# The inner weight's blocks are turned before their norm is summed, and all instructions stand in a new order

## The chip, the cores and the metric

The kernel runs on one core of a Trainium2 chip. The core has five engines that work side by side: PE (TensorE, matrix products), DVE (VectorE), ACT (ScalarE), POOL (GpSimd), and SP (SyncE), which issues nearly all DMA transfers. Each engine executes its own list of instructions in order and waits on semaphores. The metric is the device time of one execution in microseconds.

## The reference, cut to what matters

Three stages follow one another on 2304 tokens (4 batches of 576):

```python
scores = q @ k.T / sqrt(64)               # 4 x 8 heads, 576 x 576
kth    = 32nd largest score of each row
attn   = softmax(where(scores >= kth, scores, -1e9))
x      = (attn @ v)                       # 2304 x 512
h      = x @ w_in                         # 512 -> 2048
x      = (h * sigmoid(1.702 h)) @ w_out   # 2048 -> 512
out    = (((x @ w1) * (x @ w2)) @ w3) @ w_out2   # 512 -> 1024 -> 1024 -> 512
```

The weights arrive as 64-bit floats; q, k and v as 32-bit floats.

## The kernel before

**Tiles and heads.** The tokens are cut into 18 tiles of 128. Each tile has 8 heads, so there are 144 heads (a head below is one tile by one attention head). A head has a fixed course. PE forms its 128x576 scores in one of two PSUM score buffers ("S", line 1122). DVE finds the 32nd largest score of each row by four maxima of eight values (L1142) with three replacements between them (L1145). ACT forms "cut" (L1164) out of the scores and the fourth maximum and by that frees the score buffer; then it takes the exponential (L1167). The result is split into a high and a low half of 16 bits (L1230, L1185), turned by a DMA transpose (L1188), and multiplied with v on PE (L1202, L1204). As there are two score buffers, S of a head waits for the cut of the head two before it. After 8 heads the tile goes through the two gated networks, whose products are L772 to L774: each product of two numbers is made of three 16-bit products of their halves.

**Weights.** They are 72 blocks of 128 x 512: 8 of w_out2 ("w4"), 16 of w3 (1024 x 1024, the inner weight), 16 of w_in, 16 of w_out and 16 of w1 and w2. `load64` brings one block in as 16-bit pieces of the 64-bit numbers (L487; SP), into one of six raw slots. Its highest piece is copied (the "top": ACT L499, POOL L502 or DVE L505), passed into PSUM (the "pass": PE L508 or ACT L511) and joined there with the rest to a 32-bit number by DVE (the "join", L516). The join frees the raw slot, so that the load six blocks later can go out. `l2_scale` sums up a group of blocks with PE: the "gram" (L554, four products per block), its diagonal (L565), and from it a power of two by which the group is scaled. w3 is used in two groups of 8 blocks. `split` makes the high half (L602) and the low half of a scaled block. The low half has several ways: PE takes the high half back into PSUM ("back", L611) and DVE subtracts (L618); or PE forms the difference by two matmuls ("less", L614 and L615) and ACT stores it; or ACT or POOL do it alone (L624, L627, L631).

**The inner weight.** w3 and w_out2 are multiplied together before the first tile needs them: `weights()` turns each joined block of w3 on PE (`turned3`, L683, copied by ACT at L686) and forms the product (L809). The turn waits for the join and for the block's gram, and it is the turn that gives the block's storage back.

**The order.** All operations are registered with an object `Order`, which has for each a list of alternatives (engine and code). A compressed table, `PLAN`, holds for each operation its rank and its chosen alternative; `Order.run` writes the operations out by rank. So the table sets the list of every engine, the loads of SP among them.

```python
o.rank, k = self.plan[len(self.ops)]          # L66
for o in sorted(self.ops, key=lambda o: o.rank):   # L83
```

Of the kernel before, what the change touches and what calls it, by code (L numbers as in the profile page):

```python
# [18 lines left out]
AF = mybir.ActivationFunctionType  # L19
# [18 lines left out]
class Order:  # L38
# [104 lines left out]
PE_DUE, PE_OUT = 100.0, 20.0  # L143
TURN = ("w4", "w3")
# [10 lines left out]
    'c-jq@17jUa07h3cv!mUa-J18tO`4?Xt=%SRn<i~kyGd=^wr$(CZQHiZ_x{6&a}-5YG(}ga;wYJwoQj{Pgc7ZkRG@+sQ^5*TEKdec7LUIY;0abjl`y4{Qc6iw'  # L155
    'YJ2*47I-##aw)l$5GAh?;qiIOdSW~+lt`tBQb|crs(8kE#(SoFiYsN5T1q`7U1{KH=xOTNq@*Y{l)6fDrK{4#v(0nKvrgHioKwy#SCqS+`<~~XV(NC~wsJ@L'
    'tbA3zcnmM_3PmceC##Z2iBj@=3Mv_u?4Cd+Na0E*Pc}~u#iMvV;YvQmP(T@?*h*2Qm=dp~Dm9hHo`If`N}N*1Q{U50DW@cRIxGE@Udk|Ks%M5WRGHwJ?^&cQ'
    'RhB6$JS&wE$`sFHWx3K#>8nih%u!Y=>y-_j{feqGHM2LXT3Riu#(Qh2@03r9?nP>nT32oA?W)#P)6{ft2h~wCdVSua>Qm*V^4{}PiBYR~t9k3G)s<FC8>NHN'
    'Lm8k9Rz@jfm08L><*H(;{gp||TxE;0RoS8JR*oxYm3zu7<-77%X`{APJF7j^-s)g=h&o1{psrNcsCU$7s;$0I2PqSk>&gvfvNBWoplE6~HOTwVyGq%tWKeUc'
    'zZIzFR{hm-YMi&acc-#f2~%U$1Ii&KMQx(CQoDOkdygnbm8t4H^`vr2*{WVv@2gL}nqN<~mwH{jt#(oSs-ILt<636Fv3@tyk7_0@w>C<htQOQ#w5D1szaf4}'  # L160
    'TC&zqOVh@x)70_WG;OA~)9;MmPxZIDQroBPQ7@|dwG-N7?TMc!Fs~ZnE#i$<iJD2x>CL5{P;Po|d7deM6z=tSz3N|8_~rETYBSWC-dWzc>R0ubiu`QNPYqP_'
    'c*E68>Rs<E?`!pfdP{xmeWLDHkEzGKr_}!H0ClJLpn6n2sh;(oSMRAW)i>UEYGEy2OYlq7(zV7~6TcQ(d9|WiNljF1t98@{YD2Y=+D#o+c0{Aujpj6JS9W}('
    'MU56WYF~C-*-m9Am2IvrYt*sPibnogh!&;g*9vH5v>2^|R#B_0)h*XItzKHcw9L`@{qy+y{A+6U)9R#kOsl4~OskRBI_<mqM^!alqnfK_(fqVPEuR*o6-q0X'
    '7M<3noT+!!vgm)bV!G6e>v^>DX+_iG(gtYbv`N}zZHhKqo1-n$)@diTL)vTYnD#}xT+UC2dOrPYxu0pj(tf8|(b@eo_=oySE!eMwUrB9|wo%*Uw^=K#mD8$f'
    ')wQ?k2k#dz(}rmywfWj&t(n@wJKwud?V<Jb8{{`iJFFem&iS3!DrxPs_F5+`yOv9f)QW4pwBFiqzv<d3?V@(c?~Zm=yQV$R9%|dQ9ojCxgIYJOyEa#wr#;o4'
    'YcKs?X;-wH+AZz2c2~QnJ=0!jZ?t#Xd+mevP5bx%oaj2xGwPXij~<}s)eA&d^)KyT&3}Hh9kAFxLqLh>hW@esjr`~6d!koGABYauBhq`N_f3z|E9!;x%6epU'
# [100 lines left out]
def kernel(  # L267
# [840 lines left out]
    def head(t, h, X):  # L1108
# [100 lines left out]
        if h == H - 1:  # L1209
            rel += [("q", qe, "qa"), ("q", qe, "qb")]  # L1210
# [362 lines left out]
```

## Time and profile before

| what | us |
|---|---|
| three runs | 949.43, 949.82, 950.68 |
| median | 949.82 |
| profiled execution, whole | 950.18 |
| its span in the profile | 948.4 |
| PE / DVE / ACT / POOL busy | 921.8 / 865.2 / 724.5 / 785.2 |
| granted TensorE clock, mean of the span | 0.998 of full speed |

The profiled execution lies 0.36 us above the median. The span is what the profiler shows from the first to the last instruction; 1.8 us of the execution lie outside it. PE's 26.6 us without work are the difference between its busy time and the span. Names are those of the program without buffer numbers: `w` is a raw block or a joined one, `win` and `wout` are the storage of the split weights, into which blocks are also joined early; `ysb` and `usb` are work buffers; `mm` and `s_ps` lie in PSUM.

### The profile page before, as it was taken

Reading aid. Unit: us, or ns where it says so; the run is one execution under the profiler, and the core shown is the slowest. Engines: PE = TensorE matmul, PEld = TensorE weight load, DVE = VectorE, ACT = ScalarE, POOL = GpSimd, SP = SyncE. Lnnn points to the kernel's source line nnn. Section 1 sums busy time; section 2 is a strip of 40 time slices with the busy share of each in tenths; the row PEclk is TensorE's granted clock in tenths of the full one; section 3 lists DMA queues with packets and bytes.
Section 4 is the critical chain, followed back from the end, with each engine's and each line's share of the span. In section 5 each row is a group of like instructions: output and inputs, shape, how many; then the busy total and the mean of one; then the engine's idle time right before and its main releaser. Section 6 shows DMA issues by size and latency. Waiting matters only on the chain.

```text
span 948.4 us, 19725 instructions
## 1 busy us (share of the span) xinstructions
PE 921.8 (97%) x6641; PEld 484.6 (51%) x6642; DVE 865.2 (91%) x1838; ACT 724.5 (76%) x1426; POOL 785.2 (83%) x1045
## 2 busy tenths in 40 slices
PE   4799989999999999999999999999999999999998
PEld 2555555555545555555555555554555555544553
DVE  5999999999999999999999999999999999997252
ACT  5899999998879987877888796887776676745231
POOL 3899998999989998999999998989997887856101
PEclk9999999999999999999999999999999999999999
DMA  8999999877987887878895798598675846656201
GB/s 290 321 304 332 298 232 243 180 136 139 160 159 138 163 133 138 145 140 151 142 183 110 141 172 155 100 158 169 123 124 111 161 96 129 118 94 108 44 12 45
DMA packets 397862, 149.31 MB, mean 157 GB/s; under 512 B 375872, under 2 KB 384064, under 8 KB 397760
## 3 DMA queue, kind: packets, MB, share of 16 engines
q1 hardware_dynamic: 397760, 148.05, 75.6%
q8 instruction: 52, 0.85, 0.4%
q14 instruction: 50, 0.41, 0.1%
HBM read 52.41 MB, written 4.72 MB: 60 GB/s over the span
## 4 chain that ended last, share of the span: by engine, by line
PE 82%; ACT 5%; POOL 4%; DVE 3%; DMA 3%; issue 2%; SPq 1%; ACTq 0%; POOLq 0%; DVEq 0%
PE mm L772 23%; PE mm L774 22%; PE mm L773 22%; PE s_ps L1122 7%; PE mm L1204 4%; PE mm L1202 2%; DMA w<-in_moe_w_out_dram 1%; DVE ysb L1145 1%; DVE m8s L1142 1%; ACT mm L511 1%; DMA tsb<-in_moe_w_dram 1%; DMA ysb<-in_k_dram 1%; ACT ysb L1167 1%; PE mm L614 1%; POOL wout L631 1%
## 5 line engine op out<-in xcount | busy, mean ns | idle before, releaser
L1142 DVE MAX8 m8s<-ysb 128x8 f32<-128x576 f32 x432 | 321.5, 754 | 6.3
L1145 DVE MATCH_REPLACE8 ysb<-m8s,ysb 128x576 f32<-128x576 f32 x288 | 213.9, 743 | 0.0
L1185 POOL TENSOR_TENSOR ysb<-ysb 128x512 f16<-128x512 f32 x142 | 164.3, 1160 | 0.3
L1164 ACT ACTIVATE ysb<-s_ps,m8s 128x576 f32<-128x576 f32 x144 | 106.2, 738 | 56.4 <-DVE m8s L1142 45.6
L772 PE MATMUL mm<-w,usb 128*128 128x512 f16 x377 | 142.9, 379 | 0.0
L774 PE MATMUL mm<-w,usb 128*128 128x512 f16 x377 | 142.9, 379 | 0.0
L773 PE MATMUL mm<-w,usb 128*128 128x512 f16 x377 | 142.9, 379 | 0.0
L774 PEld LDWEIGHTS <-usb 128*128 128x128 f16 x824 | 80.6, 98 | 97.2
L1167 ACT ACTIVATE ysb<-ysb,nbs,small 128x576 f32<-128x576 f32 x144 | 123.7, 865 | 5.2 <-POOL nbs L1152 2.3
L772 PEld LDWEIGHTS <-usb 128*128 128x128 f16 x824 | 80.5, 98 | 86.4 <-issue 2.6
L773 PEld LDWEIGHTS <-usb 128*128 128x128 f16 x824 | 80.6, 98 | 82.6
L1142 DVE MAX8 m8s<-s_ps 128x8 f32<-128x576 f32 x144 | 108.6, 754 | 1.8 <-PE s_ps L1122 1.5
L1145 DVE MATCH_REPLACE8 ysb<-m8s,s_ps 128x576 f32<-128x576 f32 x144 | 107.6, 747 | 0.0
L1122 PE MATMUL s_ps<-kts,qts 128*128 128x288 f16 (+1 forms) x640 | 96.7, 291 | 2.1 <-ACT ysb L1164 2.1
L772 PE MATMUL mm<-win,usb 128*128 128x512 f16 x240 | 91.0, 379 | 0.0
L774 PE MATMUL mm<-win,usb 128*128 128x512 f16 x240 | 90.9, 379 | 0.0
L773 PE MATMUL mm<-win,usb 128*128 128x512 f16 x240 | 90.9, 379 | 0.0
L774 PE MATMUL mm<-wout,usb 128*128 128x512 f16 x207 | 78.5, 379 | 0.0
L773 PE MATMUL mm<-wout,usb 128*128 128x512 f16 x207 | 78.4, 379 | 0.0
L772 PE MATMUL mm<-wout,usb 128*128 128x512 f16 x207 | 78.4, 379 | 0.0
L1122 PEld LDWEIGHTS <-qts 128*128 128x128 f16 (+1 forms) x640 | 55.3, 101 | 42.4 <-issue 13.1
L1204 PEld LDWEIGHTS <-ats 128*128 128x128 f16 (+1 forms) x1440 | 68.4, 100 | 9.3 <-issue 4.3
(305 smaller groups left out, 2107.4 us busy)
## 6 DMA issues: line engine op xcount, KB each, us to landing
w<-in_moe_w_out_dram SPq DMA_DIRECT2D x24, 511.8 KB, 5.5
w<-in_moe_w_dram SPq DMA_DIRECT2D x22, 511.8 KB, 5.9
w<-in_moe_w_in_dram SPq DMA_DIRECT2D x16, 511.8 KB, 6.3
qts<-qts SPq DMA_DIRECT2D x34, 128.0 KB, 2.5
ysb<-in_k_dram SPq DMA_DIRECT2D x16, 256.0 KB, 3.6
ysb<-in_v_dram SPq DMA_DIRECT2D x16, 256.0 KB, 2.9
out_dram<-usb SPq DMA_DIRECT2D x16, 256.0 KB, 2.9
usb<-in_q_dram SPq DMA_DIRECT2D x13, 256.0 KB, 3.5
```

Source lines behind the costliest of these rows:

```text
L511: nc.scalar.copy(E["mm"], E["w"].bitcast(BF16)[:, 0:C])
L772: nc.tensor.matmul(o, a[:, i, :], hi, start=(first and i == 0), stop=False)
L773: nc.tensor.matmul(o, a[:, i, :], lo, start=False, stop=False)
L774: nc.tensor.matmul(o, a[:, 4 + i, :], hi, start=False, stop=(last and i == 3))
L1122: nc.tensor.matmul(E["sp"][r : r + n, i], qe[q_][:, h, r : r + n], kt[:, j * S + i * HS : j * S + (i + 1) * HS], start=k_ == 0, stop=k_ == 1,)
L1142: nc.vector.max(out=E["m8"][:, 8 * i : 8 * i + 8], in_=E["sp"] if i == 0 else E["w"])
L1145: nc.vector.match_replace(out=two(E["w"]) if i == 0 else E["w"], in_to_replace=E["m8"][:, 8 * i : 8 * i + 8], in_values=E["sp"] if i == 0 ...
L1164: nc.scalar.activation(two(E["y"]), E["sp"], AF.Prelu, bias=E["m8"][:, TOPK - 1 : TOPK], scale=-1.0, alpha=1.0 / FAR)
L1167: nc.scalar.activation(E["y"], E["y"], AF.Exp, bias=E["nb"], scale=nesc)
L1185: return lambda: eng.tensor_tensor(hl()[:, S + SR : 2 * S], *y_of(at_main, SM), op=ALU.subtract)
L1202: nc.tensor.matmul(o[:, 0:D], at_, v2[:, j_, blk, 0:D], start=False, stop=False)
L1204: nc.tensor.matmul(o[:, 0 : D + 1], at_, v2[:, j_, blk, D : P + 1], start=i == 0, stop=i == 8)
```

## The change

The turn of a w3 block no longer waits for the block's gram but for its join alone. The gram now waits for the turn and gives the block back. All 16 turns are registered ahead of the grams, which is why the grams of a group can stand together behind them. Three alternatives are offered to the table beside this: k, q and the attention weights of the first batches and tiles may be turned on PE (`by_pe`) where a DMA transpose did it. The new table uses this for one transpose of k alone: nine small matmuls (L784 after) and three copies on ACT, and 14 transposes of k by DMA where there were 15. The table itself is new throughout.

```diff
+A_BOTH, Q_BOTH, K_BOTH = 5, 4, 2
@@ PLAN
-    'c-jq@17jUa07h3cv!mUa-J18tO`4?Xt=%SRn<i~kyGd=^wr$(CZQHiZ_x{6&a}-5YG(}ga;wYJwoQj{Pgc7ZkRG@+sQ^5*TEKdec7LUIY;0abjl`y4{Qc6iw'
+    'c-jq@V|yM=13;Ifo!Qx)-Mhver*WF3R@63alQvCir?!o!wr$(CZQHi(zVA;s*L6OeBT0&+Nmw!^F6EN^rMyytR7pydR0&8#G9>D?ym`F&yn#{yDbgDvg-aEr'
...
@@ l2_scale
-                0.235, due - 1000, lambda i=i: f_gram(i), deps=[prev, Es[i]["join"]], env=E, acq=["mm"] if i == 0 else [], tag="gram"
+                0.235, due - 1000, lambda i=i: f_gram(i), deps=[prev, Es[i]["join"], Es[i].get("turn")], env=E, acq=["mm"] if i == 0 else [],
+                rel=[("blk", Es[i], "w")] if "turn" in Es[i] else [], tag="gram"
...
@@ turned3
-        a = pe(0.45, 0.0, f_in, deps=[W["join"], W["gram"]], env=E, acq=["f", "mm"], rel=[("blk", W, "w")], tag="w3 in")
+        W["turn"] = a = pe(0.45, 0.0, f_in, deps=[W["join"]], env=E, acq=["f", "mm"], tag="w3 in")
...
@@ weights
+        e3 = [{} for _ in E3]
+        tr3 = [turned3(W, e) for W, e in zip(E3, e3)]
         g3 = [l2_scale(E3[8 * g : 8 * g + 8]) for g in range(2)]
...
-                e = {}
-                tr = turned3(E3[2 * f + kc], e)
+                e, tr = e3[2 * f + kc], tr3[2 * f + kc]
...
@@ kv_prep
-        last_of["k T"] = dma(
-            1.35, due, f_t, deps=[m], env=E, rel=["kh"], tag="k T", lat=2.4, data=1.40, after=last_of.get("k T")
+        both = b < K_BOTH
...
+            kready[b, hp] += by_pe([piece(0, 4), piece(4, 8), piece(8, 9)], [m, last_of["k T"]], [], [("kh", E, "kh")], "k ")
```

The numbers of lines are higher after the change: load L495, join L524, turn L692, gram L562, S L1191, maximum L1211, replacement L1214.

**SP, the first loads.** SP's list from its start; `in_moe_w_out_dram` is w_out2 here, `in_moe_w_dram` is w3, `w_70` the raw slots. Before:

```order
L1063 DMA w_70<-in_q_dram 128x8x64
L487 DMA w_70<-in_moe_w_out_dram 128x2047
L982 DMA ysb<-in_k_dram 128x2x256
L987 DMA ysb<-in_k_dram 64x64 x2
L487 DMA w_70<-in_moe_w_out_dram 128x2047 x3
L982 DMA ysb<-in_k_dram 128x2x256
L987 DMA ysb<-in_k_dram 64x64 x2
L487 DMA w_70<-in_moe_w_out_dram 128x2047 x2
```

After:

```order
L1113 DMA w_70<-in_q_dram 128x8x64
L495 DMA w_70<-in_moe_w_dram 128x2047
L1023 DMA ysb<-in_k_dram 128x2x256
L1028 DMA ysb<-in_k_dram 64x64 x2
L1023 DMA ysb<-in_k_dram 128x2x256
L1028 DMA ysb<-in_k_dram 64x64 x2
L495 DMA w_70<-in_moe_w_out_dram 128x2047
L495 DMA w_70<-in_moe_w_dram 128x2047
L1023 DMA ysb<-in_k_dram 128x2x256
L1028 DMA ysb<-in_k_dram 64x64 x2
L1113 DMA usb<-in_q_dram 128x8x64
```

The first weight is a block of w3, where the first six were blocks of w_out2. A third piece of k and the q of tile 1 (into `usb`) have moved up, and the rows after hold three weight blocks where the rows before hold six.

**PE, the turns.** The stretch around the first turns, some heads in. `w_70` and `w_71` are joined blocks, `ident` the unit matrix by which a block is turned. Before, the gram (L554) of a block stands ahead of its turn (L683):

```order
L554 LDWEIGHTS w_70
L554 MATMUL mm_91<-w_70 128x128
L683 MATMUL mm_93<-ident,w_71 128x128 x4
L554 LDWEIGHTS w_71
L554 MATMUL mm_91<-w_71 128x128
```

After, turns (L692) stand between passes (L516) ahead of a head's S (L1191), with no gram (L562) yet:

```order
L516 LDWEIGHTS ident
L516 MATMUL mm_90<-w_71,ident 128x512
L692 MATMUL mm_93<-ident,w_70 128x128 x4
L516 LDWEIGHTS ident
L516 MATMUL mm_91<-w_71,ident 128x512
L692 MATMUL mm_92<-ident,w_71 128x128 x4
L516 LDWEIGHTS ident
L516 MATMUL mm_93<-w_71,ident 128x512
L516 LDWEIGHTS ident
L516 MATMUL mm_90<-w_71,ident 128x512
L692 MATMUL mm_91<-ident,w_71 128x128 x4
```

Five turns stand ahead of the first gram of any block; before, seven blocks had their gram ahead of the first turn.

**DVE, the joins.** The stretch among the first heads' maxima, where `s_ps` is a new head's first maximum. Before:

```order
L1145 MATCH_REPLACE ysb<-m8s,ysb 128x576
L516 SCALAR_TENSOR_TENSOR w_71<-w_70,mm_90 128x512
L1142 MAX m8s<-ysb 128x8
L516 SCALAR_TENSOR_TENSOR w_71<-w_70,mm_93 128x512
L1142 MAX m8s<-s_ps_89 128x8
L516 SCALAR_TENSOR_TENSOR w_71<-w_70,mm_92 128x512
L1145 MATCH_REPLACE ysb<-m8s,s_ps_89 128x576
```

After:

```order
L524 SCALAR_TENSOR_TENSOR w_71<-w_70,mm_90 128x512
L1211 MAX m8s<-ysb 128x8
L524 SCALAR_TENSOR_TENSOR w_71<-w_70,mm_91 128x512
L1214 MATCH_REPLACE ysb<-m8s,ysb 128x576
L524 SCALAR_TENSOR_TENSOR w_71<-w_70,mm_90 128x512
L1211 MAX m8s<-ysb 128x8
L524 SCALAR_TENSOR_TENSOR w_71<-w_70,mm_93 128x512
L1211 MAX m8s<-s_ps_88 128x8
L524 SCALAR_TENSOR_TENSOR w_71<-w_70,mm_90 128x512
```

After, the joins stand closer: in 32 rows of DVE's list from the first one shown there are 13 of them, where 32 rows from the first one shown before hold 10.

## Rows read from the trace of the kernel before

**Rows 1.** Part 1 of the page: engine, busy us, share of the span, instructions.

```profile
PE 921.8 (97%) x6641; PEld 484.6 (51%) x6642; DVE 865.2 (91%) x1838; ACT 724.5 (76%) x1426; POOL 785.2 (83%) x1045
```

**Rows 2.** Windows: length; busy PE, PEld, DVE, ACT, POOL; clock; DMA share; GB/s.

```profile
0.00:24.00 24.00, 10.75 (x56) 5.57 (x57) 13.02 (x30) 12.81 (x26) 9.57 (x21) 1.00 0.90 290
24.00:192.00 168.00, 158.43 (x1042) 89.29 (x1043) 163.65 (x381) 161.01 (x318) 154.67 (x207) 0.99 1.03 272
192.00:900.00 708.00, 708.00 (x5297) 368.02 (x5296) 669.13 (x1398) 537.85 (x1062) 615.11 (x811) 1.00 0.74 135
900.00:948.40 48.40, 44.60 (x248) 21.74 (x246) 19.39 (x31) 12.86 (x22) 5.85 (x7) 1.00 0.11 28
```

**Rows 3.** The same view for the first full stretch of heads.

```profile
24.00:48.00 24.00, 19.36 (x124) 13.85 (x124) 23.68 (x56) 21.47 (x46) 20.81 (x28) 0.93 1.04 323
```

**Rows 4.** Timeline 179:184: start, length, engine, line, operation; in brackets its wait.

```profile
179.19 1.41 DVE L1142 MAX8 m8s<-ysb 128x8 f32<-128x576 f32 x2
...
181.14 0.72 ACT L1164 ACTIVATE ysb<-s_ps,m8s 128x576 f32<-128x576 f32 x1
...
181.91 0.65 PE L1122 MATMUL s_ps<-kts,qts 128*128 128x288 f16 x4 [0.20 <-ACT ysb L1164]
...
182.67 0.77 DVE L1142 MAX8 m8s<-s_ps 128x8 f32<-128x576 f32 x1 [0.63 <-PE s_ps L1122]
```

**Rows 5.** Waits of DVE from 17 to 190 us: total, times, longest.

```profile
DVE msm L1303 <- ACT usb L1288: 0.9, 2, 0.7
DVE small L1295 <- ACT small L1294: 0.8, 1, 0.8
...
DVE m8s L1142 <- PE s_ps L1122: 0.6, 1, 0.6
```

**Rows 6.** Timeline of PE, 119.5:121, the gram of two blocks.

```profile
120.01 0.39 PE L554 MATMUL mm<-w 128*128 128x128 bf16 x4
120.24 0.39 PE L554 MATMUL mm<-win 128*128 128x128 bf16 x4
```

**Rows 7.** Timeline of PE, 129:133, preparation of the weights.

```profile
131.00 1.02 PE L614 MATMUL mm<-win,tsb 128*128 128x512 f32 x2
131.86 0.38 PE L615 MATMUL mm<-w,ident 128*128 128x512 f16 x1
132.08 0.38 PE L611 MATMUL mm<-win,ident 128*128 128x512 f16 x1
```

**Rows 8.** DVE by line and form: out<-in, count, busy us, mean ns.

```profile
L1142 DVE MAX8 m8s<-ysb 128x8 f32<-128x576 f32 x432 | 321.5, 754 | 6.3
L1145 DVE MATCH_REPLACE8 ysb<-m8s,ysb 128x576 f32<-128x576 f32 x288 | 213.9, 743 | 0.0
...
L516 DVE SCALAR_TENSOR_TENSOR wout<-w,mm 128x512 uint32<-128x512 uint32 x25 | 16.7, 677 | 0.3 <-issue 0.2
...
L618 DVE SCALAR_TENSOR_TENSOR win<-win,small,mm 128x512 f16<-128x512 f32 x4 | 3.0, 739 | 0.1
...
L426 DVE SCALAR_TENSOR_TENSOR usb<-xsb,msm,usb 128x512 f16<-128x512 f32 x1 | 0.8, 751 | 0.9 <-ACT usb L416 0.9
```

**Rows 9.** Timeline 15:18, up to the first maximum.

```profile
15.58 0.66 ACT L499 CAST w<-w 128x512 f16<-128x512 bf16 x1 [1.07 <-DMA w<-in_moe_w_out_dram]
...
16.90 0.69 DVE L516 SCALAR_TENSOR_TENSOR w<-w,mm 128x512 uint32<-128x512 uint32 x1 [0.74 <-ACT mm L511]
...
17.51 0.76 DVE L1142 MAX8 m8s<-s_ps 128x8 f32<-128x576 f32 x1
```

**Rows 10.** Timeline 910.5:911.2, two engines reading SBUF together.

```profile
910.65 1.19 POOL L1324 TENSOR_TENSOR usb<-psb,usb 128x512 f16<-128x512 f32 x1 [11.71 <-ACT usb L1318]
910.86 1.53 DVE L1324 TENSOR_TENSOR usb<-usb 128x512 f16<-128x512 f32 x1
```

**Rows 11.** Timeline of DVE, 870.5:870.6, the same operation alone.

```profile
870.55 0.69 DVE L1324 TENSOR_TENSOR usb<-usb 128x512 f16<-128x512 f32 x1
```

**Rows 12.** Part 6 of the page: one weight block's load, KB, us to landing.

```profile
w<-in_moe_w_dram SPq DMA_DIRECT2D x22, 511.8 KB, 5.9
```

More of the change, by code (lines that the diff above doesn't have):

```diff
@@ L159 @@
[L159 to L166, printed above, removed]
@@ L252 @@
+    'OVbh'
 )
@@ L763, in turns, with by_pe, f_pe, f_a @@
         return res
+    def by_pe(banks, deps, acq, rel, tag):
+        none = ("N", 0.0, None, 0.0)
+        prev, res = deps[-1], []
+        for k_, (mats, view, dst, n) in enumerate(banks):
+            T = {}
+            def f_pe(T=T, mats=mats):
+                todo = mats(T["b"])
+                for i, (o, w_) in enumerate(todo):
+                    nc.tensor.matmul(
+                        o, w_, upper(ident)[0 : w_.shape[0], 0 : w_.shape[0]], start=i == 0 or (i == 1 and o.shape[0] < P), stop=i == len(todo) - 1, skip_group_check=True
+                    )
+            def f_a(T=T, view=view, dst=dst):
+                nc.scalar.copy(dst(), view(T["b"]))
+            def f_v(T=T, view=view, dst=dst):
+                nc.vector.tensor_copy(dst(), view(T["b"]))
+            c = 0.03 + 0.055 * n * (1 if len(mats.__defaults__ or ()) < 2 else mats.__defaults__[1]) / P
+            prev = op(
+                [none, ("T", c, f_pe, 0.0), ("T", c, f_pe, 0.0)], 0.0, deps=deps + [prev],
+                acq=(list(acq) if k_ == 0 else []) + [("mm", T, "b")], rel=rel if k_ == len(banks) - 1 else [], tag=tag + "turn",
+            )
+            k = n / C
+            res.append(op(
+                [none, ("A", 0.1 + 0.38 * k, f_a, 0.0), ("V", 0.08 + 0.52 * k, f_v, 0.0)], 0.0, deps=[prev], rel=[("mm", T, "b")], tag=tag + "turned",
+            ))
+        return res
     def product_op(due, get, at, w, blocks, first, last, deps, acq, rel, tag):
@@ L1209, in head @@
         if h == H - 1:
-            rel += [("q", qe, "qa"), ("q", qe, "qb")]
+            rel += [("q", qe, x) for x in (("qa", "qb", "qap", "qbp") if qe.get("both") else ("qa", "qb"))]
         s = pe(0.49 if len(pt) == 1 else 0.62, due - 1000 - 8, f_s, deps=qhalf[t, h // 4] + kd + [last_of.get("S")], env=E, acq=["sp"], rel=rel, tag="S")
@@ L1243, in head, with part, mats @@
         else:
-            tr = [dma(1.35, due + 8, f_t, deps=[lo], env=E, acq=["at"], rel=["hl"], tag="a T", lat=2.4, data=1.40, after=last_of.get("a T"))]
+            both = t < A_BOTH
+            none = ("N", 0.0, None, 0.0)
+            tr = [op([("D", 1.35, f_t, 0.0)] + [none] * (2 * both), due + 8, deps=[lo], env=E, acq=["at"], rel=["hl"], tag="a T", lat=2.4, data=1.40, after=last_of.get("a T"))]
+            if both:
+                def part(i0, i1):
+                    def mats(t_):
+                        return [(t_[:, (i - i0) * P : (i - i0 + 1) * P], hl()[:, i * P : (i + 1) * P]) for i in range(i0, i1)]
+                    return mats, lambda t_: t_[:, 0 : (i1 - i0) * P].rearrange("p (k m) -> p k m", m=P), lambda: E["atp"][:, i0:i1], (i1 - i0) * P
+                tr += by_pe([part(0, 4), part(4, 8), part(8, 9)], [lo, tr[0]], [("at", E, "atp")], [("hl", E, "hl")], "a ")
+                E["both"] = True
         last_of["S"], last_of["a hi"], last_of["a T"] = s, hi, tr[0]
@@ L1250, in head @@
                 0.845 if len(pt) == 1 else 1.0, due - 1000 + 10, f_av, deps=X["tr", h - 1] + tr + [last_of.get("av")] + vd,
[L1251 removed]
+                acq=[("mm", X, ("av", hp))] + ([("x", X, "x")] if hp == 0 else []), rel=[("at", z, k_) for z in (X["E", h - 1], E) for k_ in (("at", "atp") if z.get("both") else ("at",))] + rel, tag="av",
             )
```

225 lines of the change are left out of this document (131 added, 94 removed).

## The prediction

> **What bounds the kernel now.** I read part 1 of the page first. PE works 921.8 us of a span of 948.4 [rows 1], so 26.6 us of idle PE are all that an order can give back without taking work away. The windows say where these lie [rows 2]: 13.25 us in the first 24, 9.57 in the 168 up to 192, none at all in the 708 from there to 900, and 3.80 in the tail. From about 192 on PE is never out of work, so the end is set by two things: when that state is reached, and how much PE work is then left.
>
> What holds PE up before is read from the timeline around its last wait [rows 4]. S of the 23rd head starts at 181.91 and waited for the cut of the 21st, which frees a score buffer. The cut started at 181.14, though DVE had ended the 21st head's fourth maximum at 179.9 (the first of the two at 179.19, half of 1.41 each): a hand-off of 2.0 us, mostly ACT busy with other things. DVE then took up the new scores at 182.67 after 0.63 of waiting. DVE works 163.65 of the 168 us of that window [rows 2], and 23.68 of the first 24 of them, while PE works 19.36 [rows 3]; its waits between 17 and 190 are few, the largest 0.9 for ACT in two pieces, 0.8 for ACT, 0.6 for S [rows 5]. So up to the 23rd head the heads go at DVE's pace, and PE fills the gaps between the S of one head and the next with weight work. PE work moved ahead of that S is hidden; PE work moved behind it is paid in full.
>
> **The sum, at the S of the 23rd head.** I count instructions ahead of it in both orders and price them from the trace.
>
> PE ahead of that S. A 128x512 product of 16 bits takes 0.22 (131.86 to 132.08), a "less" of three matmuls 1.08 (131.00 to 132.08) [rows 7]; a small 128x128 matmul 0.057, by the eight of two grams (120.01 to 120.24 for four) [rows 6]. After the change there are 9 small matmuls more for k (+0.51), 8 backs fewer (-1.73), 2 lesses fewer (-2.16), 7 passes more (+1.51) and six matmuls fewer of a tile product (-1.30): -3.17 us. Over the whole program PE has 8 passes more (+1.73), 8 backs fewer (-1.73), one less fewer (-1.08) and the 9 small ones: -0.57. So behind that S there are 2.60 us more PE work than before: +2.6 on the end, if S comes at the same time. The 3.17 taken from the front only make longer gaps there.
>
> DVE ahead of that S, from its first maximum of all to the fourth of the 21st head, with the work before it: 2 maxima more at 0.754, 2 replacements more at 0.743, 2 joins fewer at 0.677, 7 subtractions behind a back fewer at 0.739, and 3 subtractions more that read both operands from SBUF, at 0.751 of the one such row [rows 8]; with a 0.72 and a 0.74 more of the first gate and the inner product, one 0.68 of turned q fewer and some small ones (-0.27, estimates by the same rows): 1.51 + 1.49 - 1.35 - 5.17 + 2.25 + 0.78 - 0.27 = -0.8. It is not all gain, for ACT and POOL take over what DVE gives up; I take -0.6.
>
> The start. The first maximum comes at 17.51, directly behind a join at 16.90 [rows 9]. Before the change 6.29 us of DVE work lie ahead of it, after it 5.61. The early w3 block stands behind 3.5 MB of loads. In the trace a top that waited for its load stood behind 3.75 MB and started at 15.58 [rows 9]; 3.5 MB in proportion to the 323 GB/s of the stretch behind [rows 3] are 0.8 earlier, about 14.8 to 15.2. From there top, pass and join take 1.9 (15.58 to 17.51), so the maximum comes at 16.7 to 17.2 with 0.68 less work done: +0.4, with 1 us to either side.
>
> The hand-off of 2.0 us can lose up to 1.2 when ACT is free at the fourth maximum, or stay; ACT's order there is new. I take the middle, -0.6.
>
> DVE's waits for ACT. ACT has some 4 to 5 us less work around the heads of tile 1: 15 of the small operations behind a maximum leave it, 4 tops and 8 passes, while 11 more scalings for low halves join it elsewhere. The two rows of waiting for ACT are 1.7 together [rows 5]. The ends are -2.0 (all of it and a little of the start) and +2.0 (the new order opens as many again); I take -1.2, near the row, since the work that made them late gets less.
>
> Two engines at one memory. Three more subtractions of DVE in front read both inputs from SBUF. Beside a POOL operation of the same kind, DVE's took 1.53 [rows 10]; alone, 0.69 [rows 11]. So each costs between nothing and 0.84, together 0 to 2.5. POOL is busy 154.67 of 168 us [rows 2], but much of that is not of this kind; I take 0.5. The Trainium skill ("GPSIMD Engine Reference", section 1, Specifications, row SBUF interfaces) says that POOL shares its SBUF interfaces with DVE and contends with a DVE instruction that has two SBUF inputs. By that rule, which these two rows agree with, the replaced subtractions, which read PSUM, were free of it, and the change buys shorter PE work at the price of a shared port; this is rival C.
>
> What the new wait costs by itself. The gram now waits for the turn, and on PE both stand in one list, so it is never late by that. The turn waits for a join alone; a late join would hold the passes and the S queued behind it on PE. Where the five turns stand, PE has 4.6 of 24 us to spare [rows 3], and I take nothing; if that cover is gone it is the time of one join, 0.7. A block's storage comes back later, by the gram: nothing as long as joins find storage, else part of rival B. The transposes that move from the DMA queues to PE take nothing off the path: one of 15.
>
> Sum: 2.6 - 0.6 + 0.4 - 0.6 - 1.2 + 0.5 = +1.1 us. Against the profiled execution of 950.18 that gives 951.3; this one stands 0.36 over the median of the runs, so against the median it is 949.82 + 1.1 = 950.9.
>
> **Rivals.** A, the front's idle PE is what is paid. PE idles 4.6 us between 24 and 48 [rows 3] while the clock is down to 0.93 of its full 2.4 GHz there, and turns that wait only for a join could fill this. Then the heads aren't the limit but the weights' preparation, and a shorter one moves the whole plan forward: for it, that all turns and sums of w3 lie in this stretch; against it, that DVE is full (23.68 of 24) and holds each S. If three quarters of the 4.6 and the hand-off's 0.6 are won, 949.82 - 4.1 = 945.7.
>
> B, the loads run dry. The DMA engines are full in the same stretch (a share of 1.04 at 323 GB/s [rows 3]; 1.03 up to 192 [rows 2]). There are six raw slots, and a load goes out only when the join six blocks before is done; one takes 5.9 us to land [rows 12]. After the change 13 joins stand in 32 rows of DVE's list where 10 did. At one join per 1.05 us (12 in some 12.6 us of DVE work, by the prices above), six slots turn over in 6.3: just above 5.9 plus the top and the pass of 1.3 (15.58 to 16.90 [rows 9]), which makes 7.2. So each turn of the slots can come 0.9 late, or for the 13 joins two turns, and the joins stand in DVE's list ahead of maxima: 1.8, and as much again when k, v and q transfers lie between. It decides when DVE waits at a join for a pass. 950.9 + 3.6 = 954.5, slower. Against it: before the change the joins waited for no load after 17 us [rows 5].
>
> C, the shared port. All three cost 0.84, and the POOL operations beside them as much, which delays the low halves of the attention weights: 950.9 + 2.0 + 0.7 = 953.6.
>
> **How the numbers follow.** The forecast has 0.50, A 0.25, B 0.13, C 0.12. A measurement of this kernel tells about 0.2%, 1.9 us, from no change: faster means below 947.9, slower above 951.7. The forecast's own range, by its bounds on start, hand-off and waits, is 948.5 to 953.4; of its 0.50 about 0.04 falls below 947.9, 0.29 between, 0.17 above. A gives 0.22 to faster and 0.03 to the same, B 0.12 to slower and 0.01 to the same, C 0.09 and 0.03. Together: faster 0.26, same 0.36, slower 0.38. The range takes in half of A's cases and nearly all of B's and C's: 946.3 to 954.6.
>
> **What would show it.** In the profile after: PE's busy time 921.2; no PE idle between 192 and 900, so that the difference of the times is the difference of the idle time in front plus -0.57; the last wait of an S (L1191) for a cut near the 23rd head, within 2 us of 181.9; the first maximum (L1211) at 16.7 to 18.5; DVE waiting for ACT under 1 us between 17 and 190. Rival A would show the last such S before 179 with PE's idle in front under 20 us; B, DVE at a join (L524) waiting for a pass whose top waits for its load; C, DVE's rows of L434 at 1.3 us or more. The forecast is wrong at its root if S stops waiting for cuts much earlier or later than the 23rd head, for then the PE work that is counted as paid is another.

## The result, and the profile after

The changed kernel takes 955.81 us (median of 955.40 to 956.20) against 949.75 before in the same comparison: the ratio is 1.0054, with a 95% interval of 1.0040 to 1.0069. It is slower: by the medians 6.1 us, by the ratio 5.1 (3.8 to 6.6), where 1.1 was forecast, and it lies over the upper end of the range. Its profiled execution took 955.99 us, with a span of 954.0.

Part 1 of the page of the kernel after, then its windows, in the columns of [rows 1, 2]; behind them the stretch of [rows 3].

```profile
PE 924.5 (97%) x6648; PEld 484.9 (51%) x6648; DVE 861.7 (90%) x1840; ACT 721.6 (76%) x1406; POOL 789.9 (83%) x1047
```
```profile
0.00:24.00 24.00, 10.26 (x56) 5.88 (x56) 10.98 (x26) 15.50 (x34) 9.58 (x21) 1.00 0.93 264
24.00:192.00 168.00, 157.28 (x1012) 87.46 (x1013) 164.38 (x378) 157.34 (x299) 150.15 (x204) 1.00 0.99 271
192.00:900.00 708.00, 706.94 (x5314) 367.37 (x5311) 667.50 (x1409) 535.90 (x1053) 617.94 (x810) 1.00 0.74 135
900.00:954.00 54.00, 50.03 (x274) 24.20 (x271) 18.84 (x30) 12.88 (x22) 12.27 (x14) 1.00 0.11 30
```

The same view for 24 to 48 us:

```profile
24.00:48.00 24.00, 18.25 (x90) 11.29 (x90) 23.63 (x50) 18.10 (x38) 19.90 (x29) 1.00 0.96 315
```

PE's busy time has grown by 2.7 us, but not its work. A matmul of 128x512 lasts 0.38 us in the trace and the next one starts 0.22 after it; whenever PE stops, the difference counts as busy. It is better to go by starts: each matmul is given the distance to the next start that it has in an unbroken run (0.216 for 128x512, 0.057 for a gram's), and what is over is a stop. Worked out so from all of PE's records, both kernels have the same work, 912.1 and 911.8 us, and the stops grow from 28.6 to 34.2: the 5.6 us by which the spans differ. (The sums of stops shrink by 6 to 7 us behind the 28th head in both kernels, since some groups run closer than the nominal distance; only the differences between the kernels are read here. PE's work at a lower clock counts as a stop too: before has a granted clock of 0.50 from 35.2 to 38.5 us, after has 1.00 all through the front.) Where they grow, by the S of a head:

| S of head | before: start, work so far, stops | after: start, work so far, stops | stops more |
|---|---|---|---|
| 4 | 35.45, 9.07, 22.61 | 37.39, 8.39, 25.08 | 2.5 |
| 10 | 78.74, 49.11, 25.86 | 80.79, 44.19, 32.67 | 6.8 |
| 14 | 109.23, 77.67, 27.79 | 114.68, 75.58, 35.18 | 7.4 |
| 18 | 144.59, 108.67, 32.15 | 145.46, 104.81, 36.73 | 4.6 |
| 23 | 181.91, 143.06, 35.09 | 182.63, 140.12, 38.58 | 3.5 |
| 28 | 210.99, 171.63, 35.59 | 211.46, 167.18, 40.36 | 4.8 |
| last matmul | 944.22, 912.10, 28.56 | 949.65, 911.76, 34.19 | 5.6 |

So the stops grow up to the 10th head. That doesn't make all of the 6.8 us there a delay: S of the 10th head comes only 2.05 later (80.79 against 78.74), and the rest stands in the same rows as 4.9 us of PE work that the new order doesn't list ahead of that S (44.19 against 49.11). Up to the 23rd head part of it is made up, 2.1 more stops come behind that, and as 2.9 us less work is listed ahead of that S (140.12 against 143.06), 2.6 more are left behind it. The waits of PE from 15 to 82 us show what the early stops are, first of the kernel after, then of before (total, times, longest).

```profile
PE s_ps L1191 <- ACT ysb L1233: 3.1, 5, 0.9
PE mm L1035 <- ACT v2s L1032: 2.3, 2, 1.6
PE mm L516 <- POOL w L510: 1.6, 2, 1.3
PE mm L692 <- ACT kvinv L1048: 1.5, 1, 1.5
PE mm L1035 <- ACT kts L762: 1.1, 1, 1.1
PE mm L516 <- ACT w L507: 1.1, 1, 1.1
```
```profile
PE mm L994 <- ACT v2s L991: 4.2, 2, 3.8
PE mm L508 <- ACT qts L753: 1.3, 1, 1.3
PE mm L570 <- DVE wout L516: 1.1, 1, 1.1
```

Before, no S waits for a cut in this stretch. After, five do: the heads come late from DVE, and in PE's list the passes and turns stand behind the S. Two things make DVE late. First, it starts later. Its waits in the first 24 us, of the kernel after and then of before:

```profile
DVE small L1127 <- ACT usb L1116: 6.5, 2, 6.0
DVE kvc L1044 <- PE mm L1035: 2.8, 3, 1.8
DVE usb L474 <- ACT usb L469: 2.2, 1, 2.2
DVE ysb L1214 <- POOL ysb L438: 0.8, 1, 0.8
```
```profile
DVE small L1077 <- ACT usb L1066: 5.8, 1, 5.8
DVE w L516 <- ACT mm L511: 3.0, 2, 2.2
DVE kvc L1003 <- PE mm L994: 1.3, 1, 1.3
DVE w L516 <- PE mm L508: 0.7, 2, 0.4
```

Second, its list has subtractions with two SBUF operands ahead of the early heads (L434, the L426 of before). The DVE groups of that line, by form; then one of them in the timeline. It starts while the cut at 27.18 is still running, so it doesn't hold up the S behind that cut; it holds up DVE's next maximum, at 28.93:

```profile
L434 DVE SCALAR_TENSOR_TENSOR usb<-usb,small 128x512 f16<-128x512 f32 x3 | 3.5, 1168 | 0.0
...
L434 DVE SCALAR_TENSOR_TENSOR ysb<-ysb,kvc 128x576 f16<-128x576 f32 x3 | 2.7, 896 | 0.0
...
L434 DVE SCALAR_TENSOR_TENSOR usb<-xsb,msm,usb 128x512 f16<-128x512 f32 x1 | 0.7, 743 | 0.0
```
```profile
27.18 0.74 ACT L1233 ACTIVATE ysb<-s_ps,m8s 128x576 f32<-128x576 f32 x1
...
27.68 0.79 POOL L437 TENSOR_SCALAR ysb<-ysb,kvc 128x640 f32<-128x640 f32 x1
27.78 1.23 DVE L434 SCALAR_TENSOR_TENSOR usb<-usb,small 128x512 f16<-128x512 f32 x1
...
27.97 1.12 PE L1191 MATMUL s_ps<-kts,qts 128*128 128x288 f16 x4 [0.71 <-ACT ysb L1233]
...
28.93 0.75 DVE L1211 MAX8 m8s<-ysb 128x8 f32<-128x576 f32 x1
```

Counted over DVE's records up to the cut of the 4th head (48.32 us before, 52.26 after): DVE was idle 2.1 us longer (13.39 against 11.30) and had 1.8 us more work in front, of which the two subtractions are 2.08. Together that is the 3.94 us by which this cut is late.

### The profile page after: what moved, and what is told of

Its sections match the earlier page's. It is cut to its first block, busy times and chain, and to the rows that moved or that the text cites. A ratio compares the mean times of both kernels' runs of the same rounds, so it can differ in the third digit from the quotient of the medians.

```text
span 954.0 us, 19765 instructions
## 1 busy us (share of the span) xinstructions
PE 924.5 (97%) x6648; PEld 484.9 (51%) x6648; DVE 861.7 (90%) x1840; ACT 721.6 (76%) x1406; POOL 789.9 (83%) x1047
## 4 chain that ended last, share of the span: by engine, by line
PE 78%; ACT 8%; DMA 5%; DVE 3%; issue 2%; POOL 0%; SPq 0%; ACTq 0%; DVEq 0%; POOLq 0%
PE mm L812 22%; PE mm L814 22%; PE mm L813 22%; PE s_ps L1191 6%; PE mm L1274 4%; PE mm L1272 2%; DMA w<-in_moe_w_in_dram 2%; DMA w<-in_moe_w_dram 1%; DVE ysb L1214 1%; DMA tsb<-in_moe_w_dram 1%; DVE m8s L1211 1%; ACT ysb L1236 1%; ACT ysb L1233 1%; ACT wout L611 1%; ACT mm L519 1%
## 5 line engine op out<-in xcount | busy, mean ns | idle before, releaser
L1211 DVE MAX8 m8s<-ysb 128x8 f32<-128x576 f32 x432 | 320.9, 754 | 5.6
L1214 DVE MATCH_REPLACE8 ysb<-m8s,ysb 128x576 f32<-128x576 f32 x288 | 213.8, 743 | 0.0
L812 PE MATMUL mm<-w,usb 128*128 128x512 f16 x345 | 130.8, 379 | 0.0
L814 PE MATMUL mm<-w,usb 128*128 128x512 f16 x345 | 130.7, 379 | 0.0
L813 PE MATMUL mm<-w,usb 128*128 128x512 f16 x345 | 130.7, 379 | 0.0
L814 PEld LDWEIGHTS <-usb 128*128 128x128 f16 x740 | 72.3, 98 | 87.4
L812 PEld LDWEIGHTS <-usb 128*128 128x128 f16 x740 | 72.3, 98 | 77.8 <-issue 3.0
L1211 DVE MAX8 m8s<-s_ps 128x8 f32<-128x576 f32 x144 | 108.5, 753 | 2.0 <-PE s_ps L1191 1.4
L813 PEld LDWEIGHTS <-usb 128*128 128x128 f16 x740 | 72.3, 98 | 73.6
L1214 DVE MATCH_REPLACE8 ysb<-m8s,s_ps 128x576 f32<-128x576 f32 x144 | 107.6, 747 | 0.0
L1191 PE MATMUL s_ps<-kts,qts 128*128 128x288 f16 (+1 forms) x640 | 97.0, 291 | 3.7 <-ACT ysb L1233 3.5
L812 PE MATMUL mm<-wout,usb 128*128 128x512 f16 x219 | 83.0, 379 | 0.0
L814 PE MATMUL mm<-wout,usb 128*128 128x512 f16 x219 | 83.0, 379 | 0.0
L813 PE MATMUL mm<-wout,usb 128*128 128x512 f16 x219 | 83.0, 379 | 0.0
L1191 PEld LDWEIGHTS <-qts 128*128 128x128 f16 (+1 forms) x640 | 55.4, 101 | 44.7 <-issue 16.2
L1405 POOL TENSOR_TENSOR usb<-usb 128x512 f16<-128x512 f32 x61 | 70.8, 1163 | 4.0 <-ACT usb L1399 2.9
L1274 PE MATMUL mm<-v2s,ats 128*128 128x65 f16 (+1 forms) x1440 | 73.1, 194 | 0.1
L814 PE MATMUL mm<-win,usb 128*128 128x512 f16 x176 | 66.7, 379 | 0.0
```

Of the source, the lines that this page charges most:

```text
L812: nc.tensor.matmul(o, a[:, i, :], hi, start=(first and i == 0), stop=False)
L813: nc.tensor.matmul(o, a[:, i, :], lo, start=False, stop=False)
L814: nc.tensor.matmul(o, a[:, 4 + i, :], hi, start=False, stop=(last and i == 3))
L1191: nc.tensor.matmul(E["sp"][r : r + n, i], (qe[q_ + "p"] if qe.get(q_) is None else qe[q_])[:, h, r : r + n], kt[:, j * S + i * HS : j * S ...
L1211: nc.vector.max(out=E["m8"][:, 8 * i : 8 * i + 8], in_=E["sp"] if i == 0 else E["w"])
L1214: nc.vector.match_replace(out=two(E["w"]) if i == 0 else E["w"], in_to_replace=E["m8"][:, 8 * i : 8 * i + 8], in_values=E["sp"] if i == 0 ...
```

## The experiments

Each run was timed five rounds beside the kernel before; "over before" is the ratio less one, times the median of before in that comparison. "Spliced" means the operations in the order of one kernel up to a given S, and the rest in the order of the other. In the runs with a new table the turn and the gram of a block may come in either order, and the later one gives the block back. One trace is one execution: of six runs whose edit stands behind the 10th head, five have its S 0.2 to 0.7 us later than the trace of before, and the sixth, b_front12, 1.9. Shifts of that size in a single trace prove little.

| run | ratio (95%) | over before, us |
|---|---|---|
| fB_rA | 1.0051 (1.0039 to 1.0063) | 4.8 |
| fA_rB | 1.0128 (1.0111 to 1.0144) | 12.2 |
| fB29_rA | 1.0084 (1.0070 to 1.0098) | 8.0 |
| fB9_rA | 1.0067 (1.0055 to 1.0080) | 6.4 |
| fA9_rB | 1.0106 (1.0089 to 1.0122) | 10.1 |
| b_turnfirst | 1.0084 (1.0069 to 1.0100) | 8.0 |
| a_sumfirst | 1.0256 (1.0235 to 1.0278) | 24.3 |
| b_swap7 | 0.9999 (0.9989 to 1.0009) | -0.1 |
| b_front12 | 1.0011 (1.0003 to 1.0020) | 1.0 |
| b_back12 | 1.0022 (1.0013 to 1.0031) | 2.1 |
| b_join4 | 1.0004 (0.9993 to 1.0015) | 0.4 |
| b_early4 | 1.0019 (1.0010 to 1.0028) | 1.8 |
| b_early10 | 1.0069 (1.0057 to 1.0081) | 6.6 |
| a_lo_pool | 1.0120 (1.0105 to 1.0135) | 11.4 |
| a_lo_zero | 1.0045 (1.0032 to 1.0058) | 4.3 |
| a_k_dma | 1.0051 (1.0040 to 1.0063) | 4.8 |
| b_late3 | 1.0053 (1.0039 to 1.0066) | 5.0 |
| b_maxfirst | 1.0010 (1.0000 to 1.0020) | 1.0 |

**Where PE and DVE work is paid.** Three runs of before with work added: 12 passes twice, 12 first matmuls of products twice, 4 late joins twice.

```diff
+            for _ in range(2 if no in TWICE else 1):     # b_front12; b_join4 alike, at the join
                 nc.tensor.matmul(E["mm"], upper(ident), E["w"].bitcast(BF16)[:, 0:C], start=True, stop=True)
...
+                if tag == "h" and i == 0 and TWICE[0] <= due < TWICE[1]:     # b_back12
+                    nc.tensor.matmul(o, a[:, i, :], hi, start=True, stop=True)
```

b_front12: 

> Before, with 12 of the passes of weight blocks on PE between the 11th and 18th head done twice: 12 x 0.216 = 2.6 us more PE work in front. Theory (PE waits for the heads there, so its work in front is hidden): 949.8 to 950.8 us. Rival (all PE work counts, wherever it stands): 952.4.

b_back12: 

> Before, with the first matmul of 12 products of the first network in tiles 8 to 10 done twice: the same 2.6 us of PE work, behind the 23rd head. Theory (paid in full there): 952.2 to 952.6 us. Rival (hidden by DVE's pace there too): 949.8.

b_join4: 

> Before, with 4 joins among the 16th to 19th head done twice: 4 x 0.68 = 2.7 us more DVE work in front. Theory (DVE sets the pace of the heads there): the S of the 23rd head comes 2 to 2.7 us later and the end with it, 951.5 to 952.6 us. Rival (PE or ACT sets the pace): 949.8 to 950.3.

Behind the 23rd head the 2.6 us of PE are paid, 2.1 (1.2 to 2.9). In front they cost 1.0 (0.3 to 1.9). The two intervals overlap, and the trace of b_front12 doesn't show the passes to cost anything: its S of the 10th head is 1.9 late, ahead of the first added pass at 95.8 us, and that of the 23rd 1.3. Whether work in front is hidden wholly or in part stays open. The four joins cost 0.4 (-0.7 to 1.4) where 1.7 to 2.8 were expected: among the 16th to 19th head DVE had slack left, which filled up. In the window 144 to 192 its busy time rises, first before, then b_join4:

```profile
144.00:192.00 48.00, 46.44 (x342) 24.66 (x342) 46.74 (x108) 47.22 (x94) 44.09 (x57) 1.00 0.94 209
```
```profile
144.00:192.00 48.00, 46.19 (x343) 24.41 (x342) 47.90 (x112) 47.01 (x93) 44.12 (x59) 1.00 0.93 205
```

So "DVE sets the pace up to the 23rd head" was too wide. For the first heads the same edit was made with earlier joins:

```diff
-TWICE = (56, 60, 62, 66)
+TWICE = (7, 8, 13, 14)                             # b_early4
+TWICE = (7, 8, 9, 10, 11, 12, 13, 14, 15, 26)      # b_early10
```

b_early4: 

> Before, with 4 joins among the 2nd to 4th head done twice: 2.7 us more DVE work ahead of the 4th head's cut. Theory (DVE paces the early heads): the heads 5 to 14 come 2 to 2.7 us later; then before's stall of PE at 123 to 127 us (3.8 us in the window 120 to 144, for the k and v of the second batch) swallows part of it: the end 0 to 1.5 us later. Rival (not DVE): heads and end unmoved.

b_early10: 

> Before, with 10 joins among the 2nd to 5th head done twice: 6.8 us more DVE work in front, as much as the new order's heads are late at the 10th (7 us). Theory (DVE paces the early heads, the stall at 123 to 127 gives back at most 3.8): heads 6 to 14 come 6 to 7 us later, the end 2.5 to 5 us later. Rival (lateness in front is all swallowed, the loss of after is made elsewhere): within 1 us of before.

There nearly every microsecond comes out at the end: 2.7 us of joins put the S of the 10th head 2.6 later, that of the 23rd 2.3, and the end 1.8 (1.0 to 2.7); 6.8 us give 6.6, 5.8 and 6.6 (5.4 to 7.7). The later stall of before swallows almost nothing, against what I expected. The granted clock fell to 0.60 between 24 and 48 us in b_early10 and to 0.69 in b_early4 (0.93 before); b_swap7 below had 0.77 and lost nothing, so it is not the main price, though a part isn't excluded. The kernel after had 1.00 there: its loss isn't the clock's. The window 24 to 48 of b_early10:

```profile
24.00:48.00 24.00, 15.90 (x106) 12.57 (x106) 23.52 (x49) 16.52 (x34) 16.37 (x22) 0.60 1.04 286
```

DVE is as full as before (23.52 against 23.68 us).

**The subtractions.** In a_lo_pool POOL forms the six low halves of k, v and q (and their high halves) as before; in a_lo_zero DVE only writes zeros.

```diff
-                nc.vector.scalar_tensor_tensor(l, x, sc, h, op0=ALU.mult, op1=ALU.subtract)
+                nc.vector.memset(l, 0.0)           # a_lo_zero
```

a_lo_pool: 

> After, with the six low halves of k, v and q that it forms on DVE from two SBUF operands (and their high halves) back on POOL as before. DVE has 5 such operations less ahead of the 23rd head, about 5 us in the trace of after. Theory (DVE's pace sets that S, and they took longer beside POOL): 951 to 954 us. Rival (POOL, busy 90% there, becomes the limit instead): 955.8 or more. Rival (contention is nothing): 955.8.

a_lo_zero: 

> After, with the seven low halves that DVE forms from two SBUF operands (k, v, q, 6 of them in front) set to zero by DVE instead, so they are left out of the result; each takes perhaps 0.2 us in place of 0.85 to 1.23. Theory (DVE's list sets the early heads; two of them, 2.1 us, stand ahead of the 4th head's cut): heads 4 to 12 come 1.5 to 2 us earlier and the end 1.5 to 3 us earlier than after, 4 to 5 us over the median of before falls to 2 to 4.5. Rival (the early heads are late by loads and the k and v chain): as after, 6 us over before.

The zeros take 0.27 to 0.30 us each, so up to the 4th head's cut about 1.5 us go. The 10th head's S comes 1.2 us earlier than in after, the 23rd's 1.3, and the span is 952.9 against 954.0. The times say 4.3 over before against 5.1 for after, with intervals that overlap, so this rests on one trace, and is not shown beyond that. On POOL they cost more than on DVE: the tops and products then wait. The longest wait of PE for a top is 3.3 us in a_lo_pool (1.3 in after), and at 195 us it stood 2 for a product's input. In the 3.4 us from 196 on, the granted clock was 0.50. Two rows of PE's waits in a_lo_pool:

```profile
PE mm L516 <- ACT w L507: 3.3, 1, 3.3
...
PE mm L813 <- ACT usb L1440: 2.0, 1, 2.0
```

**The named edit.** b_swap7 puts the gram of seven blocks directly behind their turn; b_turnfirst moves the turns up ahead of the grams; a_sumfirst moves after's grams up to their joins; a_k_dma undoes the transpose of k on PE. Their edits lie in the table; what they do to PE's list, in short:

```diff
-gram(block), turn(block)                    # order of PE before
+turn(block), gram(block)                    # b_swap7, where the turn stood; b_turnfirst, where the gram stood
...
-join(block), ..., turn(block), ..., gram(block)      # order of after
+join(block), gram(block), ..., turn(block)           # a_sumfirst
```

b_swap7: 

> Before, with the gram of seven w3 blocks put directly behind the block's turn, at the place where the turn stood (the named edit alone, with nothing else moved). Theory: the same PE work in the same place, within 0.7 us of before. Rival (turn before sum costs by itself, as the spliced run b_turnfirst could be read): 2 us or more over before.

b_turnfirst: 

> The order of before; alone the turn of each w3 block is moved up to stand directly ahead of the block's gram, which is now behind it. Theory: turn and gram together are the same PE work and all of it lies ahead of the S of the 23rd head, so no change: 949 to 951 us. Rival (turning first is what costs, by holding storage and sums back): 952 us or more. Rival (turning first gives PE work early and gains): 948 or less.

a_sumfirst: 

> The order of after; alone the gram of each w3 block is moved up to its join, ahead of the turn where that can be. Theory: the same, no change against after: 955 to 957 us. Rival (grams held behind the turns are what starves the front of PE work): 953 us or less.

a_k_dma: 

> After, with the one transpose of k that it makes on PE done by DMA as before. Theory (its 0.5 us of PE work and three copies on ACT lie in the front, where PE waits for DVE's pace): as after, 5 to 6 us over before. Rival (it holds up S and ACT where they are late): 2 us or more below after.

In place, turning before summing costs nothing. With turn or gram moved up in the list it costs 8 us over before and 19 over after. In a_sumfirst the grams then stand in PE's list where their joins aren't done yet, and S and passes queue behind them. In b_turnfirst the turns wait 1.7 us for joins, and a gram 1.6 for ACT's copy of a turn; where the rest of its 8 us goes is not shown. The waits of PE, 15 to 82 us, in b_turnfirst, and then in a_sumfirst:

```profile
...
PE mm L693 <- DVE wout L524: 1.7, 2, 1.0
PE mm L562 <- ACT usb L696: 1.6, 1, 1.6
```
```profile
PE mm L562 <- DVE wout L524: 4.2, 2, 2.2
PE mm L562 <- DVE w L524: 3.3, 2, 2.3
```

My expectation there took equal work in the same stretch to be an equal time; it isn't. The transpose of k makes no difference that can be told from after.

**What is listed where.** b_late3 moves three half products behind the S of the 28th head; the spliced runs take both orders apart.

```diff
-x2 (8), b (1), x2 (9), S of the 28th head             # order of PE before
+S of the 28th head, x2 (8), b (1), x2 (9)             # b_late3
```

b_late3: 

> Before, with three half products of tiles 0 and 1 (two x2 and one b, 3 x 1.3 = 3.9 us of PE work) moved from just ahead of the S of the 28th head to just behind it, where after has them. New theory (the cut of the 26th head fixes when that S can start, so PE idles in their place and they are paid behind it): 2.5 to 3.9 us slower than before. Rival (PE has its backlog by then and a move within it costs nothing): within 0.7 us of before.

fB_rA: 

> The order of before up to the S of the 23rd head, the order of after from there; the k transpose of the change goes by DMA as before. Theory (the time is set by when that S comes and by the PE work that is left behind it): S of the 23rd head at 181.9 us as before, PE work left about 769 us as before, PE idle behind it like after's 1 to 2 us: 949.5 to 951.5 us. Rival (the loss is made by the new order behind that S): 953 us or more. Rival (the loss is made in front alone, nothing behind): 949.8.

fA_rB: 

> The order of after up to the S of the 23rd head, the order of before from there. Theory: S at 182.6 us and 2.6 us more PE work left, so 3.3 us over before, and up to 1 us of idle PE behind it: 953 to 954.5 us. Rival (the loss is made behind that S): 951 or less. Rival (all of it in front): 955.8.

fB9_rA: 

> The order of before, its loads and joins among it, up to the S of the 9th head, the order of after from there. New theory (the work listed behind the 28th head is after's): 955 to 957 us. Rival (the new order of loads and joins at the start is what costs): 949.5 to 952.

fA9_rB: 

> The order of after up to the S of the 9th head (its w3 block loaded first, its early turns and crowded joins), the order of before from there. New theory (the work listed behind the 28th head is before's, 740.5 us, and the heads catch up): 949.5 to 952.5 us. Rival (the start costs, the 2.8 us that the 9th head is late stay): 953 to 956.

fB29_rA: 

> The order of before up to the S of the 29th head, the order of after from there. New theory (the heads keep their pace in all these orders, so the S of the 28th head comes at 211 to 212 us; the end is that time plus the PE work listed behind it, 740.5 us in before and 744.6 in after, less some 2 to 3 us; idle PE in front is only what is left over): as before, 949.5 to 951.5 us. Rival (the rest of the new order is what costs, as the run with the cut at the 23rd head could also be read): 954 us or more.

In b_late3 the S of the 28th head stands open for 2.9 us, and PE has nothing else:

```profile
206.81 0.65 PE L1192 MATMUL s_ps<-kts,qts 128*128 128x288 f16 x4
210.34 0.88 PE L1192 MATMUL s_ps<-kts,qts 128*128 128x288 f16 x3 [2.87 <-ACT ysb L1234]
```

The first matmuls behind that stop, and the window around them:

```profile
211.25 0.63 PE L813 MATMUL mm<-win,usb 128*128 128x512 f16 x1
211.67 0.63 PE L814 MATMUL mm<-win,usb 128*128 128x512 f16 x1
```
```profile
210.30:213.40 3.10, 3.06 (x10) 1.31 (x10) 3.10 (x9) 0.49 (x1) 3.02 (x4) 0.51 1.28 157
```

2.5 to 3.9 us were expected, and 5.0 (3.7 to 6.3) measured. In the trace S of the 28th head comes 0.65 earlier than before and S of the 29th 5.58 later. The 3.9 us moved, less the 0.65, are 3.25 of this. After the stop the granted clock is 0.51, its lower level of 1.2 GHz, and PE's matmuls of 128x512 start 0.42 apart instead of 0.22: 1.4 us more, the S among it. A wait of 0.7 for ACT makes up most of what is left.

So there is no backlog on PE in the stretch that [rows 2] show without idle time: between two S's it has just the work that the order lists there, and heads and PE run at nearly the same pace. With before's order up to the 29th head, PE waits at two S's behind the seam, because their stretch of the list has been thinned. In fA_rB it is no S but a gram that waits, behind the 23rd head:

```profile
PE s_ps L1192 <- ACT ysb L1234: 4.3, 2, 2.1
```
```profile
PE mm L562 <- DVE usb L1489: 5.5, 1, 5.5
```

Every splice lost 5 to 12 us, whichever order came first, with waits of its own around the seam: one S for 1.7 us in fB_rA, a pass for 3.6 in fB9_rA, a gram for 3.0 in fA9_rB. After the stops in fB29_rA and fA_rB the granted clock was 0.50 for over 3 us. So none of them tells which part of the new order is at fault; the theory that the PE work left behind the 28th head fixes the end fell with fB29_rA (950 expected, 8.0 over before measured).

**An attempt to gain.** b_maxfirst puts four early joins behind the fourth maximum that they stood ahead of.

```diff
-join, fourth maximum
+fourth maximum, join
```

b_maxfirst: 

> Before, with four joins that stand directly ahead of the fourth maximum of the 2nd, 3rd, 4th and 6th head moved directly behind it: these cuts come 0.68 us earlier, DVE's total is the same. Theory (the total of DVE's list sets the pace, so one piece earlier is the other later): within 1 us of before. Rival (only what stands ahead of the fourth maximum counts): 1.4 to 2.7 us faster.

It costs 1.0 (0.0 to 1.9), within 1 us of before as expected: nothing is gained by having these cuts ahead of the joins. The granted clock was 0.76 from 24 to 48 us, and its part in this isn't known. No run beat the kernel before.

## Why the prediction was wrong

- **PE work behind the S of the 23rd head, +2.6.** Right: by starts it is 769.05 us before and 771.63 after, 2.6 more.
- **That S itself.** The other terms (-0.6, +0.4, -0.6, -1.2, +0.5) had it 1.5 us earlier than before; it came 0.7 later, at 182.63. That is the first failed step, 2.2 us, and it lies in DVE's idle time, not in its work. Up to the cut of the 21st head DVE had 1.0 us less work than before (165.44 against 166.44), where the sum has 0.1 less with the shared port; but it was idle 1.7 us longer (16.41 against 14.70), where the terms for start and waits make it 0.8 less. The start was mis-sized: the first maximum came at 18.22 as the range allowed, but with 0.54 us less work done and with 0.8 of waiting for POOL after it; DVE was idle 2.1 us longer up to the 4th head's cut, for the +0.4 of the sum. (The working of that term gives -0.1 to +0.4, so it took the late end of its own reading and was still too small.) The waits of DVE for ACT didn't shrink: from 18 to 184 us four joins wait for ACT's pass, 2.4 in all. The hand-off, for which 0.6 less was taken, stayed nearly as long: 1.8 against 2.0, by the same reading of the rows at 180.09 and 182.63 below.
- **Two engines at one memory.** The subtractions with `usb` took 1.17 on the mean, and two that stand between the 21st head's fourth maximum and the 23rd's first 1.04 and 1.15; the one at 895 us took 0.74. The three that I counted took 0.85, 1.23 and 1.12 where the sum has 0.751 each, so 0.9 more in all, inside the bounds, where I had taken 0.5. The rows around the S of the 23rd head:

```profile
180.09 1.41 DVE L1211 MAX8 m8s<-ysb 128x8 f32<-128x576 f32 x2
...
180.69 1.16 POOL L636 TENSOR_TENSOR wout<-w,wout 128x512 f16<-128x512 f32 x1 [0.47 <-ACT w L633]
...
181.42 1.04 DVE L434 SCALAR_TENSOR_TENSOR ysb<-ysb,kvc 128x576 f16<-128x576 f32 x1
...
181.84 0.73 ACT L1233 ACTIVATE ysb<-s_ps,m8s 128x576 f32<-128x576 f32 x1
181.94 1.04 POOL L510 TENSOR_SCALAR w<-tsb 128x512 f16<-128x512 bf16 x1
...
182.38 1.15 DVE L434 SCALAR_TENSOR_TENSOR usb<-usb,small 128x512 f16<-128x512 f32 x1
182.40 0.38 PE L516 MATMUL mm<-win,ident 128*128 128x512 bf16 x1
...
182.63 0.65 PE L1191 MATMUL s_ps<-kts,qts 128*128 128x288 f16 x4
...
183.45 0.75 DVE L1211 MAX8 m8s<-s_ps 128x8 f32<-128x576 f32 x1
```

  In both, a POOL instruction was running when the subtraction began. The Trainium skill ("GPSIMD Engine Reference", section 1, Specifications) says that DVE instructions with two SBUF inputs contend with POOL for the SBUF interfaces that they share. These rows agree with it.
- **No stop of PE behind that S.** The second failed step, 2.1 us. I took the last wait of before for the last wait of after. After, S of the 23rd head doesn't wait at all: PE works right up to it, and the cut that it needs ends 0.06 before it (181.84 and 0.73 in the rows above). But S of the 26th still waits, at 200.49, far outside the 2 us around 181.9 that the forecast allowed; by its own sign it was wrong at its root. From 192 to 900 PE is idle for 1.06 us where it was never idle before. There are 1.2 us more stops than before up to the 33rd head; the remaining 0.9 come later, among them one of PE for DVE at 888 us. The waits of PE after 184 us in the kernel after (before has none):

```profile
PE mm L812 <- DVE ats L730: 0.4, 1, 0.4
PE s_ps L1191 <- ACT ysb L1233: 0.4, 1, 0.4
PE mm L665 <- ACT xsb L1337: 0.3, 1, 0.3
```

- The sum of what was measured: 0.7 + 2.6 + 2.1 = 5.4 of the 5.6 us between the spans. It is an account, which has to come out whatever the cause; the causes rest on the runs above.
- **The deeper error** was to read one pace for all heads up to the 23rd and to make the sum at a single point. The runs show the price of DVE work to depend on where it stands: nearly in full ahead of the first heads, 0.4 for 2.7 us among the 16th to 19th. In front the new order puts more on DVE; what it takes off (the subtractions behind a back, L618) lies later, where it earns less.
- **Rivals.** A failed: idle PE in front grew. C's mechanism was there, at less than half its price, and its sign (rows of 1.3 us or more) didn't come. B came near in its price, 954.5, and in part in its mechanism: joins waited for passes. But none before 45 us for more than 0.3, when 2.5 us of the stops were already made.
- What stays open: how the lateness of the first ten heads (2.05 us of the 6.8) divides between DVE's late start, its subtractions, and tops that waited for loads (1.6 and 1.1 in the list of PE's waits). The first two are counted for the 4th head's cut; no run varied the order of loads without a seam. And no run took the kernel after back to before's time: the nearest, a_lo_zero, stays 4.3 over it.

## What to carry to other kernels

An engine without idle time in the profile need not have a backlog: in lists that run in order it may have exactly what stands between two waits, and a piece of work moved past the next wait then leaves an idle gap here and still has to be done there. In b_late3 the lower clock behind the gap came on top. Price added work on the pacing engine by its place, not by the mean: early, ahead of the first results, it came out at the end nearly in full. And make the sum at several points, the last of them behind the point where the new order itself stops waiting.

## What the runs showed of the hardware

Two of the seven subtractions on DVE with two operands in SBUF ran with no POOL instruction beside them: 0.74 us for 128x512 (at 895 us) and 0.80 for 128x576 (at 255). The other five began while a POOL instruction was running. It still had 0.24, 0.69, 0.58, 0.43 and 0.60 us to go, and they took 0.05, 0.49, 0.38, 0.24 and 0.41 longer than those two: each time some 0.2 less than POOL had left. Writing zeros over the same output took 0.27 to 0.30.

After PE had stood for 2.9 us in b_late3, the granted clock was 0.51 from 210.3 to 213.4 us, and matmuls of 128x512 started 0.42 apart instead of 0.22.
